# Attention and mixture layer on one core: key columns shared between neighbouring blocks, identities built on chip, second part of the masks loaded later

## The chip, the cores and the metric

The kernel runs on one core of one Trainium2 chip. The metric is the device time of one execution in microseconds (us). A core has a matrix engine (PE, with its weight loads shown as PEld), a vector engine (DVE), a scalar engine (ACT), a general engine (POOL), and a queue engine (SP) that mostly issues DMA transfers. DMAs are issued here by SP, by ACT and by POOL; all of them run on the same 16 DMA engines.

## The reference, cut to what matters

An attention over 8 sequences of 576 positions with 8 heads of 64 channels, followed by a gated layer on the 4608 tokens. Heads 0 to 3 see the last 32 positions, heads 4 to 7 every fourth of the last 128.

```python
def _attn_ref(q, k, v):                       # q, k, v: (8, 8, 576, 64)
    window, dilation = 32, 4
    scores = scale * np.matmul(q, k.transpose(0, 1, 3, 2))
    rel = pos[:, None] - pos[None, :]
    mask_plain = (rel >= 0) & (rel < window)
    mask_dil = (rel >= 0) & (rel < window * dilation) & (rel % dilation == 0)
    ...
    scores = np.where(masks[None], scores, -1000000000.0)
    attn = softmax(scores)
    return np.matmul(attn, v)

def _moe_ref(x, w_gate, w_val, w_out):        # x: 4608 x 512, w_gate and w_val: 512 x 1536, w_out: 1536 x 512
    g = x @ w_gate
    return (silu(g) * (x @ w_val)) @ w_out
```

## The kernel before, in words

**Packs.** The attention is cut into 46 packs. A pack is one pair of heads and up to 512 tokens, cut into blocks of 32 queries. The keys that a block can see are the 32 positions of its own and the 32 before (in steps of four for the dilated heads), so each block reads 64 neighbouring key columns, and blocks that follow each other overlap by 32. `Pack.__init__` lays out the columns of a pack: first the queries, 32 columns a block, then the keys. For each run of blocks (one run for plain heads, four for dilated ones, one for each residue) it keeps 32 more key columns than there are queries. At the start of a sequence the 32 positions before do not exist; their columns hold zeros, and the mask hides them. `cols` is the pack's width, `QKB` the widest (1152 columns), and `qkb`, the array in DRAM, has rows of `QKB` 4-byte columns. `FQ` and `QKB` also set the sizes of buffers, and all buffers that lie behind them.

**Masks and identities.** `masks` holds a 128x128 identity in 16-bit form (`ident16`) and 13 mask tiles of 64 columns. A pack adds the mask to its scores by a matmul of `ident16` with its four mask tiles. `near` marks the first 8 tiles with the identity; those are all that packs 0 to 3 read. `idents` holds two 128x128 identities in 32-bit form, one plain and one with its columns permuted; PE transposes use them (`turn_e`, `turn_y`).

**The start.** Packs 0 to 3 are worked on before any of the layer. Their keys and values lie spread over the partitions with zeros between, so that one matmul serves two heads: `first_qk` loads the queries of a pack (L349, from SP), sets the two halves of its keys to zero (L351), and loads each half into every second partition (L352: one half from SP, one from POOL). `first_v` does the same with the values (L359, L360). The order in which SP, POOL, DVE and ACT issue all this is the order of the code (`manual_schedule`). SP: queries and keys of pack 0, of pack 1, identities (L592), queries and keys of pack 2, values 0, weights unit 0 (`w_load`, L227), values 1, queries and keys of pack 3, values 2, weights unit 1, values 3, weights units 2 to 5. ACT: masks near (L590), a first Exp that loads its table (L593), the rest of the masks (L594). POOL: the zeros and the loads of the second halves, in the same order of packs.

A second list (`"Q0 S0 Q1 Y2 ..."`) gives the order of the work itself on PE, DVE, ACT and POOL. For pack m: `Q` scores (L366 the mask, L370 the blocks), `S` maximum and shift (L377, L378), `X` exponentials (L437), `T` transposes (L441), `K` a copy by ACT (L447), `A` results with the values (L389), `N` normalisation (L396 to L398), `U` transposes back (L475), `H` and `L` the high and low parts of the layer's input (L502, L505). `Y` runs matmuls of no use that keep PE busy, as `idle` does at L583. `W` prepares the weights, unit by unit: `E` (L237) and for some units `T` (L254) on ACT, `T` (L257) and `B` (L264, L267) on DVE, `H` (L275) on ACT, `L` (L279) on POOL.

**The layer.** The first 1536 tokens go through it in three chunks of 512: gate and value products (`gv_mm`, L515), tanh (L524), the gating (L529, L534), output products (L552). The attention of later packs and the preparation of the weights run between. The other 3072 tokens go through a scheme with seven products for eight (L841), whose pieces are mixed, written to DRAM and read again.

Of the kernel before, what the change touches and what calls it, by code (L numbers as in the profile page):

```python
# [18 lines left out]
P = 128  # L19
D = 64  # L20
S = 576
DIL = 4
# [12 lines left out]
BQ = 32  # L35
# [30 lines left out]
class Pack:  # L66


    def __init__(self, chunk, pair, lo, hi):
        self.chunk, self.pair = chunk, pair  # L70
        self.step = DIL if pair >= 2 else 1
        blocks = []
        width = 0
        while lo < hi:
            b, q0 = divmod(lo, S)
            n = min(S - q0, hi - lo)
            per = n // self.step
            nb = -(-per // BQ)
            if self.step == 1:
                blocks += [(b, q0 + BQ * t, BQ, width + BQ * t) for t in range(nb)]  # L80
            else:
                blocks += [(b, q0 + r + DIL * BQ * t, min(BQ, per - BQ * t), width + BQ * ((nb + 1) * r + t))
                           for t in range(nb) for r in range(DIL)]
            width += BQ * (nb + 1) * self.step
            lo += n
        groups = [blocks[a:a + 4] for a in range(0, len(blocks), 4)]
        names = {(1, 0, 0, 0): "a", (0, 0, 1, 0): "b", (1, 1, 1, 1): "F", (0, 0, 0, 0): "o"}
        kinds = "".join(names[tuple(int(q < BQ * self.step) for _, q, _, _ in x)] for x in groups)
        turn = next(n for n in range(len(groups)) if kinds[n:] + kinds[:n] in KINDS)
        self.mask = KINDS.index(kinds[turn:] + kinds[:turn])  # L90
        groups = groups[turn:] + groups[:turn]
        nq = BQ * len(blocks)
        self.groups = [[(b, q, n, BQ * (4 * g + j), nq + k) for j, (b, q, n, k) in enumerate(x)]
                       for g, x in enumerate(groups)]
        self.ng = len(self.groups)
        self.cols = nq + width
        self.order = int(self.step > 1)
        self.runs = []
        for g, x in enumerate(self.groups):
            col, first, n = P * g, S * x[0][0] + x[0][1], sum(y[2] for y in x)  # L100
            if self.runs:
                c, f, k = self.runs[-1]
                if c + k == col and f + k == first:
                    self.runs[-1] = c, f, k + n
                    continue
            self.runs.append((col, first, n))
# [18 lines left out]
NPK = len(PACKS)  # L125
# [4 lines left out]
def block_masks():  # L130

    i, j = np.arange(BQ)[:, None], np.arange(BK)[None, :]
    seen = (j > i) & (j <= i + BQ)
    f, o = [np.where(x, 0.0, NEG) for x in (seen & (j >= BQ), seen)]
    m = dict(o=[o] * 4, F=[f] * 4, a=[f, o, o, o], b=[o, o, f, o])
    return np.concatenate([np.concatenate(m[x]) for x in KINDS], axis=1)


@with_exitstack
def attention_moe(ctx, tc, qkb, vb, w, masks, ident, out):  # L140
    nc = tc.nc
    NS = NPLAIN * NF

# [24 lines left out]
    def at(o, n, dt=F32):  # L168

        assert o % 8 == 0  # L170
        key = o, n, dt
        if key not in named:
            k = n * 4 // mybir.dt.size(dt)
            named[key] = nc.alloc_sbuf_tensor_at(f"at{o}_{n}_{dt.name}", [P, k], dt, offset=origin + 4 * o).ap()
        return named[key]
# [11 lines left out]
    consts = at(0, (NM * BK + P) // 2, BF16)  # L187
    ident16, mask_sb = consts[:, :P], consts[:, P:]

    idents = at(M_SMALL - 2 * P, 2 * P).rearrange("p (n c) -> p n c", n=2)  # L190
# [26 lines left out]
    def w_load():  # L217
        nonlocal loaded
        u = loaded
        n = u % 6 if u < NU - NLAST else (u + 2) % 4  # L220

        if u >= NU or raw_of.get(n, -1) >= done["B"]:
            return False
        raw_of[n] = u
        loaded += 1
        t = at(raw_at[n], 2 * WU, I32)
        last["w"] = nc.sync.dma_start(out=t, in_=w[u // 2, u % 2].bitcast(I32))  # L227
        t = t.rearrange("p (n t) -> p n t", t=2)
        wst[u] = {"lo": t[:, :, 0], "hi": t[:, :, 1]}
        return True  # L230
# [113 lines left out]
    def first_qk(m, *zero):  # L344

        t, n = early["qk"](), pk(m).cols
        k = n - FN
        tk = t[:, FN:FN + 2 * k].rearrange("p (h c) -> p h c", h=2)
        nc.sync.dma_start(out=t[:, :FN], in_=qkb[m, :, :FN])  # L349
        for h in range(2):  # L350
            zero[h].memset(tk[:, h], 0.0)  # L351
            (nc.sync, nc.gpsimd)[h].dma_start(out=tk[h::2, h], in_=qkb[m, D * h:D * h + D, FN:n])  # L352
        st[m]["qk"] = t[:, :FN], tk

    def first_v(m, *zero):
        n = 4 * FG * (D + 1)
        t = early["v"]().rearrange("p (h c) -> p h c", h=2)
        for h in range(2):
            zero[h].memset(t[:, h], 0.0)  # L359
            (nc.sync, nc.gpsimd)[h].dma_start(out=t[h::2, h], in_=vb[m, D * h:D * h + D, :n])  # L360
        st[m]["v"] = t.rearrange("p h (g c) -> p h g c", c=D + 1)
# [215 lines left out]
    near = P + 8 * BK  # L577
# [3 lines left out]
    def idle(n):  # L581
        for _ in range(n):
            nc.tensor.matmul(out=bank_x.rearrange("p (a b) -> p a b", a=4), lhsT=warm,  # L583
                             rhs=warm.unsqueeze(1).broadcast_to([P, 4, P]), start=True, stop=True)

    with tc.manual_schedule(engines={et.SP, et.Pool, et.DVE, et.Activation}):
        nc.vector.memset(ones, 1.0)
        nc.vector.memset(some, 0.0)
        first_qk(0, nc.vector, nc.gpsimd)
        nc.scalar.dma_start(out=consts[:, :near], in_=masks[:, :near])  # L590
        first_qk(1, nc.vector, nc.gpsimd)
        nc.sync.dma_start(out=idents, in_=ident.rearrange("n p c -> p n c"))  # L592
        nc.scalar.activation(out=some, in_=some, func=AF.Exp)  # L593
        nc.scalar.dma_start(out=consts[:, near:], in_=masks[:, near:])  # L594

        idle(WARM)
        first_qk(2, nc.vector, nc.gpsimd)
        first_v(0, nc.vector, nc.gpsimd)
        w_load()
        first_v(1, nc.vector, nc.gpsimd)  # L600
        first_qk(3, nc.gpsimd, nc.gpsimd)
        first_v(2, nc.vector, nc.gpsimd)
        w_load()
        first_v(3, nc.gpsimd, nc.gpsimd)
        for _ in range(3):
            w_load()
        while w_load():
            pass
# [44 lines left out]
    for m in range(M1 + 1, NPK + 1):  # L653
        c, n = divmod(m - M1 - 1, 10)
# [133 lines left out]
    kept = [[at(M_X0 + CS * (4 + 2 * k + r), CS) for r in range(2)] for k in range(2)]  # L788
# [94 lines left out]
    def n_out(ci, t, i):  # L883
        return NT * NP * ci + NP * t + i
# [47 lines left out]
    for ci in range(NC):  # L932
# [20 lines left out]
        for t in range(NT):  # L953
            if ci == NC - 1 and t == NT - 1:
                break
            for i in range(NP):
                n = n_out(ci, t, i)
# [10 lines left out]
                if ci + 1 < NC and slot > 102 and slot % 2 == 0:  # L968
                    k = (slot - 104) // 2
# [3 lines left out]
    t = NT - 1  # L973
# [9 lines left out]
def layout(q, k, v, moe_w_gate, moe_w_val, moe_w_out):  # L983
    qkb = np.zeros((NPK, P, QKB), np.float32)
    vb = np.zeros((NPK, P, 4 * NGM, D + 1), np.float32)
    vb[..., D] = 1.0
    for m, pk in enumerate(PACKS):
        for i, (b, q0, n, qc, kc) in enumerate(x for g in pk.groups for x in g):
            qt = q0 + pk.step * np.arange(n)
            kt = q0 + pk.step * np.arange(-BQ, BQ)  # L990
            a, e = int((kt < 0).sum()), int((kt < S).sum())
            for j in range(2):
                h, r = 2 * pk.pair + j, D * j
                rq = slice(j, P, 2) if m < 4 else slice(r, r + D)
                qkb[m, rq, qc:qc + n] = q[b, h, qt].T
                qkb[m, r:r + D, kc + a:kc + e] = k[b, h, kt[a:e]].T
                vb[m, r + a:r + e, i, :D] = v[b, h, kt[a:e]]
    bits = [np.ascontiguousarray(x).view(np.int64) for x in (moe_w_gate, moe_w_val, moe_w_out)]
    w = np.stack(bits[:2]).reshape(2, NK, P, NF, P)[:, list(ORDER)].reshape(2, 2, 2, P, NF, P)
    w = w.transpose(4, 3, 1, 0, 2, 5).reshape(NF, P, 2 * DM)  # L1000
    w = np.concatenate([w, bits[2].reshape(NF, P, DM)], axis=2)
    w = np.ascontiguousarray(w.reshape(NF, P, 2, WU).transpose(0, 2, 1, 3))
    masks = np.concatenate([np.eye(P), block_masks()], axis=1).astype(ml_dtypes.bfloat16)
    order = np.arange(P).reshape(DIL, BQ).T.ravel()
    ident = np.stack([np.eye(P), np.eye(P)[:, order]]).astype(np.float32)
    return dict(qkb=qkb, vb=vb.reshape(NPK, P, -1), w=w, masks=masks, ident=ident)


_INS = ["qkb", "vb", "w", "masks", "ident"]


# [14 lines left out]
```

## Time and profile before

| | |
|---|---|
| median of 3 runs | 935.71 us (935.17 to 936.23) |
| the profiled execution | 934.96 us, of which its span is 933.2 us |
| PE busy | 921.8 us (99% of the span), 8499 matmuls |
| PEld busy | 751.5 us (81%) |
| DVE, ACT, POOL busy | 639.2, 391.1, 253.8 us |
| DMA | 205.45 MB, mean 220 GB/s |
| granted clock of PE | 1.0 in the whole span |

A row of the timeline gives the start of an instruction in us from the span's start, its duration in us, engine, line, operation, what it writes and reads, and its shape; in brackets stands for how long the engine was idle before it and what ended the wait. A row of the DMA view gives queue, count and size of a group of transfers and the median time from issue to landing in us. "SPq" and "ACTq" are the times at which those engines issue a DMA. A row of the view by stretches gives the length of a stretch and the busy time of PE, PEld, DVE, ACT and POOL in it with the number of instructions, then PE's granted clock, the share of the DMA engines and GB/s.

### The profile page before, as it was taken

The page shows a single profiled execution, that of the slowest core. Times are in us where ns is not written, and L with a number is a line of the kernel's source. Part 1 is how long each engine was busy: PE and PEld are TensorE (multiplying, and loading weights), DVE is VectorE, ACT ScalarE, POOL GpSimd, SP SyncE. Part 2 cuts the span into 40 slices and gives each one's busy share as a digit, 9 for nine tenths or more (in the row PEclk, how much of TensorE's full clock was granted, in tenths as well). Part 3 has the DMA queues.
Part 4 walks back from the last instruction along what each step waited for, and adds up shares of the span by engine and source line. Part 5 has one row for each costly group of instructions (what it writes and reads, how often), then busy time and mean ns, then how long its engine had stood idle before and what let it go on. Part 6 is the DMA issues. An engine that isn't in the chain of part 4 may idle for free.

```text
span 933.2 us, 20559 instructions
## 1 busy us (share of the span) xinstructions
PE 921.8 (99%) x8499; PEld 751.5 (81%) x8499; DVE 639.2 (68%) x1055; ACT 391.1 (42%) x664; POOL 253.8 (27%) x307
## 2 busy tenths in 40 slices
PE   7999999999999999999999999999999999999998
PEld 4778788878888878888888888888888888888886
DVE  6764738668678775757669965666689745656863
ACT  4865623323334233343345643343355523334351
POOL 6655421111111212133223111222223112343320
PEclk9999999999999999999999999999999999999999
DMA  9974515667786980767777778766766686656663
GB/s 349 349 255 174 175 41 198 235 205 262 245 287 217 305 307 5 267 217 222 226 226 236 239 224 255 242 217 213 247 208 195 219 255 189 195 189 195 201 207 111
DMA packets 75533, 205.45 MB, mean 220 GB/s; under 512 B 7728, under 2 KB 22320, under 8 KB 75440
## 3 DMA queue, kind: packets, MB, share of 16 engines
q0 software_dynamic: 27728, 100.77, 34.6%
q1 hardware_dynamic: 35472, 65.16, 19.7%
q10 hardware_dynamic: 12240, 38.20, 11.9%
q8 instruction: 67, 1.10, 0.5%
q14 instruction: 26, 0.21, 0.1%
HBM read 161.64 MB, written 42.47 MB: 219 GB/s over the span
## 4 chain that ended last, share of the span: by engine, by line
PE 73%; DVE 3%; DMA 1%; issue 1%; ACT 1%; SPq 0%; ACTq 0%; DVEq 0%
PE bo L841 32%; PE bv L841 12%; PE bg L841 12%; PE bo L552 4%; PE bg L515 4%; PE bv L515 4%; PE two L457 2%; PE two L417 2%; DMA pieces<-at_float32r 1%; PE two L441 1%; PE two L475 1%; DVE at_float32r L732 0%; SPq L740 0%; DVE at_float L529 0%; DVE at_float L719 0%
## 5 line engine op out<-in xcount | busy, mean ns | idle before, releaser
L841 PE MATMUL bo<-at_float32r 128*128 128x512 f32 x1296 | 307.1, 390 | 0.0
L841 PEld LDWEIGHTS bo<-at_float32r 128*128 128x128 f32 x1296 | 242.2, 188 | 50.6
L770 POOL DMA_DIRECT2D at_float32r<-pieces x189 | 101.3, 536 | 376.7 <-PE bo L841 216.6
L804 DVE TENSOR_TENSOR at_float<-bo,at_float 128x512 f32<-128x512 f32 (+1 forms) x169 | 114.2, 684 | 104.9 <-ACT at_float L846 49.5
L804 DVE TENSOR_TENSOR at_float32r<-at_float,at_float32r 128x512 fp32r<-128x512 f32 (+1 forms) x147 | 114.0, 800 | 40.0 <-ACT at_float32r L831 27.1
L841 PE MATMUL bv<-at_float32r 128*128 128x512 f32 x486 | 129.5, 393 | 0.0
L841 PE MATMUL bg<-at_float32r 128*128 128x512 f32 x486 | 129.3, 392 | 0.0
L515 PE MATMUL bg<-at_float32r,at_float32r 128*128 128x512 f32 x432 | 106.7, 394 | 0.8 <-DVE at_float32r L505 0.4
L515 PE MATMUL bv<-at_float32r,at_float32r 128*128 128x512 f32 x432 | 107.1, 394 | 0.0
L552 PE MATMUL bo<-at_float32r,at_float32r 128*128 128x512 f32 x432 | 106.2, 394 | 0.0
L841 PEld LDWEIGHTS bv<-at_float32r 128*128 128x128 f32 x486 | 90.2, 188 | 19.0
L841 PEld LDWEIGHTS bg<-at_float32r 128*128 128x128 f32 x486 | 90.3, 188 | 18.8
L831 ACT CAST at_float32r<-at_float 128x512 fp32r<-128x512 f32 x126 | 77.0, 622 | 67.4 <-PE bv L841 21.3
L544 POOL TENSOR_TENSOR at_float32r<-at_float,at_float32r 128x512 fp32r<-128x512 f32 x36 | 48.6, 1351 | 204.8 <-PE bo L552 138.3
L515 PEld LDWEIGHTS bg<-at_float32r,at_float32r 128*128 128x128 f32 x432 | 79.9, 188 | 18.8 <-DVE at_float32r L505 1.2
L515 PEld LDWEIGHTS bv<-at_float32r,at_float32r 128*128 128x128 f32 x432 | 79.7, 188 | 17.1 <-DVE at_float L534 0.4
L552 PEld LDWEIGHTS bo<-at_float32r,at_float32r 128*128 128x128 f32 x432 | 79.7, 188 | 16.9
L867 ACT ACTIVATE at_float<-at_float 128x512 f32<-128x512 f32 x72 | 45.6, 633 | 81.7 <-DVE at_float L804 81.7
L846 ACT COPY at_float<-bg 128x512 f32<-128x512 f32 x63 | 37.0, 587 | 94.2 <-PE bg L841 94.0
L529 DVE SCALAR_TENSOR_TENSOR at_float<-at_float,bg 128x512 f32<-128x512 f32 x36 | 24.7, 686 | 66.9 <-ACT at_float L524 66.9
L279 POOL TENSOR_TENSOR at_float32r<-at_int,at_float32r 128x768 fp32r<-128x768 f32 x24 | 44.4, 1858 | 45.2 <-ACT at_float32r L275 45.2
L869 DVE SCALAR_TENSOR_TENSOR at_float<-at_float,at_float 128x512 f32<-128x512 f32 x72 | 49.4, 686 | 10.7 <-ACT at_float L867 10.6
(94 smaller groups left out, 916.4 us busy)
## 6 DMA issues: line engine op xcount, KB each, us to landing
at_float32r<-pieces POOLq DMA_DIRECT2D x189, 512.0 KB, 3.7
pieces<-at_float32r SPq DMA_DIRECT2D x126, 256.0 KB, 3.8
at_int<-w SPq DMA_DIRECT2D x24, 768.0 KB, 7.1
out<-at_float SPq DMA_DIRECT2D x35, 256.0 KB, 3.9
at_float<-vb ACTq DMA_DIRECT2D x15, 520.0 KB, 5.2
at_float<-vb ACTq DMA_DIRECT2D x20, 390.0 KB, 4.7
at_float<-qkb ACTq DMA_DIRECT2D x13, 544.0 KB, 5.7
at_float<-qkb ACTq DMA_DIRECT2D x12, 448.0 KB, 5.2
```

The lines of the kernel that those rows point to most:

```text
L279: nc.gpsimd.tensor_tensor(out=lo, in0=wst.pop(u).bitcast(F32), in1=hi, op=ALU.subtract)
L515: nc.tensor.matmul(out=bank[:, :CH], lhsT=wcol(f, o, low), rhs=x[ORDER[j]], start=n == 0, stop=n == len(ops) - 1)
L529: last["h"] = nc.vector.scalar_tensor_tensor(out=t, in0=t, scalar=1.0, in1=bank_g[:, :CH], op0=ALU.add, op1=ALU.mult)
L544: nc.gpsimd.tensor_tensor(out=hl, in0=hst[i][0], in1=hst[i][1], op=ALU.subtract)
L552: nc.tensor.matmul(out=bank_o[j][:, :CH], lhsT=wcol(f, 2 * DM + P * j, low), rhs=x, start=f == 0 and low == 0 and x is hh, stop=f == NF - ...
L770: nc.gpsimd.dma_start(out=taken[asked], in_=pieces[asked % NPIECE])
L804: engine.tensor_tensor(out=out, in0=a, in1=b, op=op)
L831: nc.scalar.copy(out=o[:, 0], in_=src)
L841: nc.tensor.matmul(out=bank, lhsT=w, rhs=x, start=first and n == 0 and t in FRESH, stop=last and n == len(ops) - 1, skip_group_check=True)
L846: nc.scalar.copy(out=kept[KEPT[t]][r], in_=banks[0][r][:, :CS])
L867: nc.scalar.activation(out=f, in_=g, func=AF.Tanh, scale=0.5)
L869: nc.vector.scalar_tensor_tensor(out=f, in0=f, scalar=1.0, in1=g, op0=ALU.add, op1=ALU.mult)
```

## The change

Three edits.

1. **Columns of keys.** The first block of a sequence no longer has 32 columns of its own for the positions before it. Its first 32 key columns are now those of whatever lies in front: the end of the run before, or, if nothing does, only for the first run of a pack that starts with a sequence, columns of its own. They hold keys that the mask hides. The widest pack goes from 1152 columns to 1056, and `QKB` with it.
2. **Identities.** The array `ident` and its load are gone. ACT makes both 32-bit identities from `ident16`, the second with a permuted access.
3. **Masks.** The second part of the masks is issued by SP behind the values of pack 3, not by ACT behind the first Exp.

```diff
@@ Pack.__init__
-            if self.step == 1:
-                blocks += [(b, q0 + BQ * t, BQ, width + BQ * t) for t in range(nb)]
-            else:
-                blocks += [(b, q0 + r + DIL * BQ * t, min(BQ, per - BQ * t), width + BQ * ((nb + 1) * r + t))
-                           for t in range(nb) for r in range(DIL)]
-            width += BQ * (nb + 1) * self.step
+
+            kept = nb if q0 == 0 else nb + 1
+            k = max(width - BQ, 0) if q0 == 0 else width
+            blocks += [(b, q0 + r + self.step * BQ * t, min(BQ, per - BQ * t), k + BQ * (kept * r + t))
+                       for t in range(nb) for r in range(self.step)]
+            width = k + BQ * (kept * self.step + nb + 1 - kept)
@@ attention_moe
         first_qk(1, nc.vector, nc.gpsimd)
-        nc.sync.dma_start(out=idents, in_=ident.rearrange("n p c -> p n c"))
         nc.scalar.activation(out=some, in_=some, func=AF.Exp)
-        nc.scalar.dma_start(out=consts[:, near:], in_=masks[:, near:])
+        nc.scalar.copy(out=idents[:, 0], in_=ident16)
+        nc.scalar.copy(out=idents[:, 1].rearrange("p (t r) -> p r t", r=DIL),
+                       in_=ident16.rearrange("p (r t) -> p r t", r=DIL))
...
         first_v(3, nc.gpsimd, nc.gpsimd)
+        nc.sync.dma_start(out=consts[:, near:], in_=masks[:, near:])
         for _ in range(3):
             w_load()
@@ layout
-    order = np.arange(P).reshape(DIL, BQ).T.ravel()
-    ident = np.stack([np.eye(P), np.eye(P)[:, order]]).astype(np.float32)
-    return dict(qkb=qkb, vb=vb.reshape(NPK, P, -1), w=w, masks=masks, ident=ident)
+    return dict(qkb=qkb, vb=vb.reshape(NPK, P, -1), w=w, masks=masks)
```

More of the change, by code (lines that the diff above doesn't have):

```diff
@@ L139, in attention_moe @@
 @with_exitstack
-def attention_moe(ctx, tc, qkb, vb, w, masks, ident, out):
+def attention_moe(ctx, tc, qkb, vb, w, masks, out):
     nc = tc.nc
@@ L1003, in layout @@
     masks = np.concatenate([np.eye(P), block_masks()], axis=1).astype(ml_dtypes.bfloat16)
-    order = np.arange(P).reshape(DIL, BQ).T.ravel()
-    ident = np.stack([np.eye(P), np.eye(P)[:, order]]).astype(np.float32)
-    return dict(qkb=qkb, vb=vb.reshape(NPK, P, -1), w=w, masks=masks, ident=ident)
-_INS = ["qkb", "vb", "w", "masks", "ident"]
+    return dict(qkb=qkb, vb=vb.reshape(NPK, P, -1), w=w, masks=masks)
+_INS = ["qkb", "vb", "w", "masks"]
 def kernel(**inputs):
```

## The prediction

> **What bounds the kernel now.** I read the page, then the view by stretches, then the waits of PE, then the timeline of the first 32 us with the DMA rows that belong to it.
>
> ```profile
> span 933.2 us, 20559 instructions
> ```
> ```profile
> 0.00:5.00 5.00, 4.00 (x10) 1.31 (x10) 3.62 (x7) 1.49 (x2) 3.54 (x10) 1.00 0.60 163
> 5.00:31.60 26.60, 21.57 (x322) 14.68 (x320) 19.94 (x35) 17.19 (x26) 14.31 (x17) 1.00 1.02 403
> 31.60:933.20 901.60, 896.18 (x8170) 735.53 (x8170) 615.62 (x1015) 372.45 (x638) 235.97 (x282) 1.00 0.66 215
> ```
> ```profile
> PE two L457 <- DVE at_float32r L489: 1.1, 3, 0.4
> PE two L441 <- ACT at_float L437: 0.7, 1, 0.7
> PE bg L515 <- DVE at_float L529: 0.4, 1, 0.4
> ```
>
> From 31.6 us on PE is busy for 896.18 of 901.60 us, at the full granted clock, and the waits of PE in that part are these three rows, 2.2 us, none of them for a DMA. So there PE is the bound, and what the change does to later loads (fewer key columns in most of 46 packs) is hidden under PE. The first 31.6 us are another matter: PE idles 26.60 - 21.57 = 5.03 us of the second stretch, and there the share of the DMA engines is 1.02, that is, they are full. Whatever comes out of this change comes out of the start, and moves all that follows by as much.
>
> How the start hangs together, from its timeline:
>
> ```profile
> 6.63 1.08 PE L370 MATMUL fs<-at_float 128*32 128x128 f32 x32 [1.19 <-DMA at_float<-qkb]
> ...
> 12.05 0.59 ACT L447 COPY at_float<-fk 128x512 f32<-128x512 f32 x1 [0.29 <-PE fk L441]
> ...
> 13.62 1.09 PE L389 MATMUL fr<-at_float,at_float 128*32 128x130 f32 x32 [1.15 <-POOL at_float L359]
> ...
> 16.11 1.09 PE L389 MATMUL fr<-at_float,at_float 128*32 128x130 f32 x32 [0.81 <-DVE at_float L398]
> ...
> 19.09 0.69 DVE L377 TENSOR_REDUCE at_float<-fs 128x8 f32<-128x512 f32 x1 [0.69 <-PE fs L370]
> ...
> 27.90 0.68 DVE L505 TENSOR_TENSOR at_float32r<-fs,at_float32r 128x512 fp32r<-128x512 f32 x1
> ...
> 31.58 0.50 PE L515 MATMUL bg<-at_float32r,at_float32r 128*128 128x512 f32 x1 [0.41 <-DVE at_float L529]
> ```
>
> The first scores wait for keys. The results of pack 0 (13.62) are put down to POOL's zeros (L359), but those had long been done; by the issue and landing rows below it is a DMA. After the results of pack 1 (16.11) PE works nearly without a gap to the scores of pack 3, whose maximum on DVE starts at 19.09; from there DVE runs without a pause to the low part of pack 3 at 27.90, after which the layer starts and PE is full from 31.58. So the end is set by how early the chain 13.62, 16.11, 19.09 runs.
>
> Issues by POOL (start, us) and the DMA rows of the same transfers (landing after so many us), in the same order: keys of pack 0, values of pack 0, values of pack 1.
>
> ```profile
> 1.69 0.67 POOL L352 DMA_DIRECT2D at_float<-qkb  x1 [0.32 <-POOL at_float L351]
> ...
> 6.55 0.54 POOL L360 DMA_DIRECT2D at_float<-vb  x1 [0.30 <-POOL at_float L359]
> ...
> 8.36 0.54 POOL L360 DMA_DIRECT2D at_float<-vb  x1 [0.29 <-POOL at_float L359]
> ```
> ```profile
> at_float<-qkb POOLq DMA_DIRECT2D x1, 160.0 KB, 4.6
> at_float<-vb POOLq DMA_DIRECT2D x1, 260.0 KB, 6.8
> at_float<-vb POOLq DMA_DIRECT2D x1, 260.0 KB, 7.5
> ```
>
> Keys 0 land at 1.69 + 4.6 = 6.29, and the scores start at 6.63. Values 0 land at 6.55 + 6.8 = 13.35, and their use starts at 13.62, although the copy that it also needs ended at 12.05 + 0.59 = 12.64. Values 1 land at 8.36 + 7.5 = 15.86, and their use starts at 16.11, together with the end of the normalisation before it. Three gates of the start are loads on full DMA engines.
>
> **The change part by part.** *The identities' load goes.* It is issued by SP right behind the keys of pack 1; both rows and their landings:
>
> ```profile
> 2.86 0.48 SPq L352 DMA_DIRECT2D at_float<-qkb  x1
> ...
> 3.38 0.59 SPq L592 DMA_DIRECT2D at_float<-ident  x1
> ```
> ```profile
> at_float<-qkb SPq DMA_DIRECT2D x1, 136.0 KB, 4.6
> ```
> ```profile
> at_float<-ident SPq DMA_DIRECT2D x1, 128.0 KB, 5.3
> ```
>
> Keys 1 land at 7.46, the identities at 8.68: on SP's queue they take up to 1.22 us, which is the upper end. The lower end is their 131 KB at the rate of a full stretch (354 GB/s, below): 0.37 us. Later issues of SP come 0.6 us earlier, which costs nothing and gives nothing, as the queue behind them is full already.
>
> ```profile
> 5.90:6.90 1.00, 0.27 (x12) 0.30 (x16) 0.24 (x1) 0.00 (x0) 0.70 (x2) 1.00 1.09 354
> ```
> ```profile
> q10 hardware_dynamic: 288, 0.25, 18.6%
> ```
>
> The second row is ACT's DMA queue in the first 4 us: both parts of the masks, 246 KB in short packets, took 0.186 x 4 = 0.74 us of all DMA engines. By that rate 131 KB cost 0.39 us. Short packets of masks are the nearest row to the short rows of the identities (512 bytes), so I take 0.39 us.
>
> *The second part of the masks moves.* It is a third of those bytes and half of the packets: 0.25 to 0.37 us less ahead of the keys and values; I take 0.25, by bytes as before. It comes back behind values 3, ahead of weights units 2 to 5: one more issue on SP (about the 0.59 us of the identities' row) and 0.25 us of DMA. Behind it wait these weights alone. They land earlier by all the rest of the sum and later by this 0.25; the exponent step on ACT waits for one of them:
>
> ```profile
> 25.83 0.94 ACT L237 ACTIVATE at_int<-at_int 128x768 f32<-128x768 f32 x1 [0.49 <-DMA at_int<-w]
> 26.66 0.56 ACT L502 CAST at_float32r<-fs 128x512 fp32r<-128x512 f32 x1
> ```
>
> The high part of pack 3 stands behind it on ACT and ends at 27.22, 0.68 us ahead of the DVE step at 27.90 that reads it. That slack covers the 0.25. If it did not, the loss would be those 0.25 us at most. The masks themselves are first read by later packs, beyond this stretch.
>
> *Fewer key columns.* Among the first four packs only 0 and 2 (dilated) shrink, by 96 columns of 4 bytes in 128 rows: 49 KB each, 98 KB together, at 354 GB/s 0.28 us. The zeros shrink as well:
>
> ```profile
> L351 DVE MEMSET at_float<- 128x640 f32 x2 | 1.2, 592 | 0.2
> ...
> L351 DVE MEMSET at_float<- 128x544 f32 x1 | 0.5, 512 | 0.1
> ```
>
> 0.08 us on DVE for each pack; POOL does its halves, so its later issues come some 0.15 us earlier. On a full queue that adds nothing to the DMA term, and I do not add it.
>
> [...] Rows of the array go from 4608 bytes (18 x 256) to 4224 (16.5 x 256), so every second row starts off a 256-byte boundary. The rows of the values have 4160 bytes, three of four off such a boundary, and the DMA rows of later packs do not show it as a loss:
>
> ```profile
> at_float<-vb ACTq DMA_DIRECT2D x15, 520.0 KB, 5.2
> ...
> at_float<-qkb ACTq DMA_DIRECT2D x13, 544.0 KB, 5.7
> ```
>
> I take nothing for it. [...]
>
> *ACT's copies.* Two copies of 128x128; the nearest row and the next thing that ACT does for the start:
>
> ```profile
> L497 ACT COPY at_float<-two 128x128 f32<-128x128 f32 x6 | 1.7, 284 | 0.0
> ```
> ```profile
> 9.22 0.63 ACT L437 ACTIVATE at_float<-at_float 128x512 f32<-128x512 f32 x1 [6.54 <-DVE at_float L378]
> ```
>
> Two such copies are 0.57 us. They wait for the near masks, which the masks' matmul on PE also needs well ahead of 6.63. Behind them on ACT stands the exponential at 9.22, with 6.54 us idle ahead of it: even copies slowed threefold by the permuted access cost nothing. Their reader, the transposes ahead of the copy at 12.05, comes later still.
>
> *Sum.* Ahead of values 0 and 1 the DMA engines have 0.39 + 0.25 + 0.28 = 0.92 us less to do. Upper end: 1.22 + 0.37 + 0.28 = 1.87, but the results of pack 0 also need the copy that ends at 12.64. That moves only with the first scores; ahead of them lie the 0.25 to 0.37 of the masks and half of the keys' 0.28, some 0.4 to 0.5 us. So the results can start at about 12.1 at best, 1.5 us earlier, and that caps the gain. Lower end: the 0.15 us of POOL's earlier issues. The later gates (values 1 at 15.86, the work of DVE from 19.09 on) move alike. I take 0.9 us. Against the profiled execution: 934.96 - 0.9 = 934.1 us. The median is 0.75 above that execution, so 935.71 - 0.9 = 934.8 us.
>
> What this measurement can tell from no change is about 0.2%, 1.9 us; so I forecast a small gain that counts as no change.
>
> **The rivals.** *POOL's queue keeps its own pace* (0.20). The gates are loads of POOL's queue, the bytes removed lie mostly on SP's and ACT's. [...] For it: values 0 take 6.8 us to land while a weights unit is under way. Against it: the engines are full, and in a full stretch work that is gone must come off something. [...]
>
> *All gates give way* (0.08). The identities' 1.22 us fall wholly to POOL's queue and the first scores move by 1 us as well, so that the cap is gone: at least 1.9 us, 933.8 or below, faster. Against it: the keys of pack 0 are issued ahead of the identities.
>
> *PE's order gets worse* (0.06). The layer's matmuls are cut into by attention work where the scheduler finds it ready, and loads of other lengths could move the cuts.
>
> ```profile
> 207.94 2.95 PE bv L515 x12
> 210.89 2.72 PE bo L552 x12
> ```
> ```profile
> 40.13 2.20 PE L515 MATMUL bg<-at_float32r,at_float32r 128*128 128x512 f32 x9
> ```
>
> Twelve matmuls take 2.72 us, and 2.95 after a cut, so a cut costs 0.23; the last row shows a set of twelve cut after nine. To be slower by over 1.9 us with 0.9 gained takes (1.9 + 0.9) / 0.23 = 13 cuts more: 937.6. Against it: 46 packs have their places in the code, and all their loads are issued long before use.
>
> **How the numbers follow.** The forecast has 0.66. Forecast and first rival stay within 0.2%: 0.86; faster 0.08; slower 0.06. The range takes in the forecast's ends (0.15 to 1.5 us gained), the first rival, and 0.5 us either way for the spread of the runs: 933.7 to 936.1.
>
> **What would show it.** Right: no transfer of identities; the first scores near 6.2, the results of pack 0 near 12.7, of pack 1 near 15.2, DVE's maximum near 18.2, and the layer's full pace from 30.7, with the same idle time of PE as before after that. The first rival shows as values 0 landing near 13.2 again. Wrong: a wait of PE behind the copies of ACT, or for the weights that stand behind the moved masks, or more than 5.5 us of idle PE after the start.

## The result and the profile after

The changed kernel took 940.60 us (median of 6 runs, 939.92 to 940.98), the kernel before 935.44 us beside it (6 runs, 934.51 to 936.23). The ratio is 1.0054, with a 95% interval from 1.0041 to 1.0067: slower by 5.2 us. The profiled execution took 940.98 us. Its page, the span and the line of the engines:

```profile
span 939.2 us, 20559 instructions
...
PE 923.2 (98%) x8499; PEld 753.0 (80%) x8499; DVE 638.6 (68%) x1055; ACT 391.7 (42%) x666; POOL 253.4 (27%) x307
```

The span grew by 6.0 us, while the count of instructions is the same. The view by stretches, with the cuts used for before (stretch and its length, then the busy time of PE, weight loads, DVE, ACT and POOL, then granted clock, DMA share and GB/s):

```profile
5.00:31.60 26.60, 18.10 (x307) 12.77 (x308) 16.38 (x29) 13.32 (x20) 12.13 (x15) 0.99 0.96 378
31.60:933.20 901.60, 898.96 (x8175) 737.42 (x8174) 617.98 (x1018) 376.28 (x643) 237.77 (x283) 1.00 0.65 214
```

In the start, PE did 18.10 us of work where before did 21.57, so it idled 8.50 us instead of 5.03. The other engines did less there too (DVE 16.38 for 19.94, ACT 13.32 for 17.19): the whole start waited for something. The timeline of the start shows where it turns from ahead to behind:

```profile
6.15 1.08 PE L370 MATMUL fs<-at_float 128*32 128x128 f32 x32 [1.34 <-POOL at_float L359]
...
13.22 1.09 PE L389 MATMUL fr<-at_float,at_float 128*32 128x130 f32 x32 [1.09 <-DMA at_float<-vb]
...
15.60 1.09 PE L389 MATMUL fr<-at_float,at_float 128*32 128x130 f32 x32 [0.70 <-issue]
...
18.57 0.69 DVE L377 TENSOR_REDUCE at_float<-fs 128x8 f32<-128x512 f32 x1 [0.69 <-PE fs L370]
18.72 1.73 POOL L279 TENSOR_TENSOR at_float32r<-at_int,at_float32r 128x768 fp32r<-128x768 f32 x1 [4.37 <-ACT at_float32r L275]
...
20.40 0.56 POOL L360 DMA_DIRECT2D at_float<-vb  x1
24.90 1.72 POOL L279 TENSOR_TENSOR at_float32r<-at_int,at_float32r 128x768 fp32r<-128x768 f32 x1 [3.94 <-ACT at_float32r L275]
...
27.32 1.09 PE L389 MATMUL fr<-at_float,at_float 128*32 128x130 f32 x32 [1.82 <-POOL at_float32r L279]
...
31.84 0.68 DVE L505 TENSOR_TENSOR at_float32r<-fs,at_float32r 128x512 fp32r<-128x512 f32 x1
...
36.44 3.02 PE L515 MATMUL bg<-at_float32r,at_float32r 128*128 128x512 f32 x12 [0.26 <-DVE at_float L529]
```

Up to 18.57 every step stands 0.4 to 0.5 us earlier than in the kernel before: the first scores at 6.15 for 6.63, the results of pack 0 at 13.22 for 13.62, those of pack 1 at 15.60 for 16.11, DVE's maximum of pack 3 at 18.57 for 19.09. Then POOL's queue holds something unexpected. POOL waits 4.37 us with nothing to do, subtracts to make the low part of weights unit 0 (L279) from 18.72, and only then issues, at 20.40, the load of the second half of values 3 (L360). In the kernel before the same load, and the results that need it:

```profile
14.79 0.54 POOL L360 DMA_DIRECT2D at_float<-vb  x1 [0.30 <-POOL at_float L359]
...
22.78 1.09 PE L389 MATMUL fr<-at_float,at_float 128*32 128x130 f32 x32
```

The rows of the load itself (KB, then us from issue to landing), before and after:

```profile
at_float<-vb POOLq DMA_DIRECT2D x1, 260.0 KB, 6.1
```
```profile
at_float<-vb POOLq DMA_DIRECT2D x1, 260.0 KB, 6.8
```

Before: issued at 14.79, landed at 20.89, used at 22.78, with 1.9 us to spare. After: issued at 20.40, landed at 27.20, used at 27.32. The results of pack 3 start 4.54 us later, although the load is 6.31 us later. The bracket of the row at 27.32 names POOL's L279, and the waits of PE repeat it:

```profile
PE fr L389 <- POOL at_float32r L279: 1.8, 1, 1.8
```

It is not L279 that ends this wait: the subtraction that ended last before it began at 24.90 and ended at 26.62, and the results started 0.12 us after the landing. A wait that names an engine long done is to be checked against the DMA rows.

Behind pack 3's results, its low part starts on DVE at 31.84 (27.90 before, 3.94 later), and the layer is at full pace, with its first set of twelve products run in one go, at 36.44 (31.58 before, 4.86 later). So another 0.92 us is lost between the two, where the stretch by single microseconds shows the granted clock (the number ahead of the DMA share):

```profile
31.00:32.00 1.00, 0.89 (x3) 0.69 (x4) 1.00 (x3) 1.00 (x2) 0.00 (x0) 0.66 0.12 49
32.00:33.00 1.00, 1.00 (x4) 0.73 (x3) 1.00 (x2) 1.00 (x2) 0.00 (x0) 0.50 0.26 25
33.00:34.00 1.00, 1.00 (x4) 0.81 (x3) 1.00 (x2) 0.86 (x2) 0.64 (x1) 0.50 0.52 117
34.00:35.00 1.00, 1.00 (x4) 0.76 (x4) 0.25 (x1) 0.26 (x1) 1.00 (x1) 0.63 1.00 418
```

The clock falls to 0.50. What is missing adds up to 0.34 + 0.50 + 0.50 + 0.37 = 1.71 us, which is 3.4 us at half clock, just where the layer's first products run; before had 1.00 there. What makes it fall there is not shown: ahead of the fall, from 28.0 to 31.3, PE was busy for 1.48 of 3.30 us at a clock of 1.00.

Of the 6.0 us of span, 4.86 are made by 36.44. The other 1.2 lie in the 900 us behind the start, which took 902.8 us here (939.2 less 36.44) and 901.6 before. It will be seen below that this part scatters by more than that from one profile to the next. In the medians 5.2 - 4.9 = 0.3 us is left.

So the load stands behind a subtraction that waits for ACT. In the code it does not. All issues of the start stand in a first list, in manual order, and the work in a second one; the load of values 3 is the last of POOL's first list, and the subtraction for unit 0 the first of its second. The order in which the built program holds POOL's instructions (number, line, operation, output and input), before:

```
20 L359 MEMSET at_2080_float_194 128x1040 x2
21 L360 DMA at_2080_float_194<-vb 64x1040
22 L279 ISA
23 L279 TENSOR_TENSOR at_1536_float32r<-at_776_int_313,at_1536_float32r 128x768
```

and after:

```
20 L359 MEMSET at_2080_float_194 128x1040 x2
21 L279 ISA
22 L279 TENSOR_TENSOR at_1536_float32r<-at_776_int_314,at_1536_float32r 128x768
23 L360 DMA at_2080_float_194<-vb 64x1040
```

Within each list the order is that of the code, but across the border between the two the program was built with the two instructions swapped. No line of the diff touches either of them.

### The profile page after: what moved, and what is told of

Read it like the earlier page. It is cut to its first block, busy times and chain, and to the rows that moved or that the text cites. A ratio compares the mean times of both kernels' runs of the same rounds, so it can differ in the third digit from the quotient of the medians.

```text
span 939.2 us, 20559 instructions
## 1 busy us (share of the span) xinstructions
PE 923.2 (98%) x8499; PEld 753.0 (80%) x8499; DVE 638.6 (68%) x1055; ACT 391.7 (42%) x666; POOL 253.4 (27%) x307
## 4 chain that ended last, share of the span: by engine, by line
PE 73%; DVE 3%; DMA 1%; issue 1%; ACT 1%; SPq 0%; ACTq 0%; DVEq 0%
PE bo L843 31%; PE bv L843 12%; PE bg L843 12%; PE bo L552 4%; PE bg L515 4%; PE bv L515 4%; PE two L457 2%; PE two L417 2%; DMA pieces<-at_float32r 1%; PE two L441 1%; PE two L475 1%; DVE at_float32r L734 0%; SPq L742 0%; DVE at_float L529 0%; DVE at_float L721 0%
## 5 line engine op out<-in xcount | busy, mean ns | idle before, releaser
L279 POOL TENSOR_TENSOR at_float32r<-at_int,at_float32r 128x768 fp32r<-128x768 f32 x24 | 43.4, 1817 | 52.5 <-ACT at_float32r L275 48.5
```

The costliest lines, as they stand in the source:

```text
L279: nc.gpsimd.tensor_tensor(out=lo, in0=wst.pop(u).bitcast(F32), in1=hi, op=ALU.subtract)
```

## The experiments

The first theory: the whole loss is this swap, made by the identities' edit, and with the order restored the three edits gain what the prediction said, or nothing. Its rivals: the loss comes from the load's place but also from the edits' other effects (ACT's copies, moved masks), or from the masks' and columns' edits.

### The order pinned

The changed kernel, with the subtraction ordered behind the last load of the first list:

```
-            (nc.sync, nc.gpsimd)[h].dma_start(out=t[h::2, h], ...)
+            last["v"] = (nc.sync, nc.gpsimd)[h].dma_start(out=t[h::2, h], ...)
...
-        nc.gpsimd.tensor_tensor(out=lo, ..., op=ALU.subtract)
+        with tc.issue_after(last["v"].ins):
+            nc.gpsimd.tensor_tensor(out=lo, ..., op=ALU.subtract)
```

> The changed kernel with one edge added on POOL: the first weights' subtraction (unit 0, low part) stays behind the load of the second half of values 3, as it was before the change. Theory 'order on POOL' (the load of values 3 is issued at 20.40 us behind the subtraction where it was issued at 14.79 before, so the results of pack 3 start at 27.3 for 22.8): the loss is gone, and the 0.5 us that the earlier steps gained are left: 934.5 to 935.3 us, faster than the kernel after by 5 to 6 us. Rival 'masks on SP' (the moved masks hold up the weights behind them): no more than 1 us better than the kernel after, about 940. Rival 'copies on ACT or columns off a 256-byte boundary': about 940 too.

Measured: 935.62 us (12 runs) beside 935.18 for before; ratio 1.0003, interval 0.9994 to 1.0012. Its timeline (lines are one higher from here on):

```profile
13.73 1.09 PE L390 MATMUL fr<-at_float,at_float 128*32 128x130 f32 x32 [1.40 <-ACT at_float L438]
...
14.63 0.54 POOL L361 DMA_DIRECT2D at_float<-vb  x1 [0.29 <-POOL at_float L360]
...
22.77 1.09 PE L390 MATMUL fr<-at_float,at_float 128*32 128x130 f32 x32
...
31.57 3.04 PE L516 MATMUL bg<-at_float32r,at_float32r 128*128 128x512 f32 x12 [0.39 <-DVE at_float L530]
```

The load is issued at 14.63 again, and all that follows stands as before, to 31.57 for 31.58. The order is the whole loss. But the gain is not there either (the 934.5 to 935.3 us expected were missed): the results of pack 0 start at 13.73, and values 0 landed at 13.49 (issued 6.39, 7.1 us later), not earlier than before's 13.35. The same kernel once more in the third set of runs:

> The pinned kernel once more, beside the two others on the same chip: 935.2 to 936, within 0.1% of the kernel before.

Measured: 935.34 us (11 runs) beside 935.21; 0.9999, 0.9990 to 1.0008. Values 0 landed at 13.19.

### The identities' edit alone, and the other two without it

The kernel before with only the second edit:

```
-        nc.sync.dma_start(out=idents, in_=ident.rearrange("n p c -> p n c"))
...
+        nc.scalar.copy(out=idents[:, 0], in_=ident16)
+        nc.scalar.copy(out=idents[:, 1].rearrange("p (t r) -> p r t", r=DIL),
+                       in_=ident16.rearrange("p (r t) -> p r t", r=DIL))
```

> Only the second edit: identities by ACT, no identities' load; columns and masks as before. In the built order of POOL the subtraction stands ahead of the load of values 3 here too. Theory 'order on POOL': slow, 939.5 to 941. Rival 'masks on SP': about 935, as the masks are not moved. Rival 'columns': about 935.

And the changed kernel with the identities loaded again (the reverse of that diff), that is, columns and masks alone:

> Only the first and third edits: shared key columns and masks' second part on SP; identities loaded as before. The built order of POOL is that of the kernel before. Theory 'order on POOL': 934.8 to 935.6, no slower than the kernel before. Rival 'masks on SP': 938 to 941. Rival 'columns off a 256-byte boundary': 938 to 941.

Measured: 940.61 us with the identities' edit alone (4 runs; 1.0054, 1.0037 to 1.0071), and 935.79 us with the other two (12 runs; 1.0004, 0.9995 to 1.0013), both beside 935.18. The load of values 3 and the layer's full pace, first with the identities' edit alone, then with the other two:

```profile
20.86 0.56 POOL L360 DMA_DIRECT2D at_float<-vb  x1
...
36.00 3.03 PE L515 MATMUL bg<-at_float32r,at_float32r 128*128 128x512 f32 x12 [0.35 <-DVE at_float L529]
```
```profile
14.64 0.54 POOL L360 DMA_DIRECT2D at_float<-vb  x1 [0.30 <-POOL at_float L359]
...
31.81 3.03 PE L515 MATMUL bg<-at_float32r,at_float32r 128*128 128x512 f32 x12 [0.39 <-DVE at_float L529]
```

One edit turns the order and loses 5 us; the other two leave it and are worth nothing that can be measured (935.79 lies just above the 934.8 to 935.6 expected).

### The kernel before with a late load

None of the edits, but the load held back until the subtraction for unit 0 is issued:

```
+            if m == 3 and h == 1:
+                held.append(t)
+            else:
...
+        "D": lambda m: nc.gpsimd.dma_start(out=held[0][1::2, 1], in_=vb[m, D:2 * D, :4 * FG * (D + 1)]),
...
-        ... U1 W4 A2 H1 ...
+        ... U1 W4 D3 A2 H1 ...
```

> The kernel before, none of the three edits, with the order on POOL turned round by hand: the load of the second half of values 3 is issued behind the first subtraction of the weights. Theory 'order on POOL': slower by 4.5 to 6.5 us, 940 to 942. Rivals: 935 to 936, as nothing else is changed.

Measured: 941.54 us (4 runs); 1.0063, 1.0043 to 1.0082.

```profile
20.38 0.57 POOL L624 DMA_DIRECT2D at_float<-vb  x1
...
27.26 1.09 PE L394 MATMUL fr<-at_float,at_float 128*32 128x130 f32 x32 [0.19 <-issue]
...
36.43 3.06 PE L520 MATMUL bg<-at_float32r,at_float32r 128*128 128x512 f32 x12 [0.22 <-DVE at_float L534]
```

Issue, use and full pace stand within 0.06 us of the changed kernel's 20.40, 27.32 and 36.44. With the pinned kernel this shows it from both sides: the late load alone makes the loss, and its removal takes all of it away.

### The copies on DVE

What in the edit turns the order? In programs that were only built, not run, the order turned whenever the identities' load left SP's queue (also when ACT issued it instead), unless the copies were put on DVE; with the load kept on SP it stayed as before. With one issue less, weights unit 0 is issued at 5.07 us (6.51 before), so a scheduler that orders by when it takes an instruction to be ready would see the subtraction sooner. The runs without a pin fit it: the order is turned where unit 0 is issued at 5.07 or 5.17 us (the latter with the identities' edit alone), and as before at 5.59 (the other two edits), 6.51 and 6.66 (the run below). That is an argument from orders, and no run shows the scheduler's reckoning. The run that goes with it, the changed kernel with

```
-        nc.scalar.copy(out=idents[:, 0], in_=ident16)
-        nc.scalar.copy(out=idents[:, 1]...
+        nc.vector.tensor_copy(out=idents[:, 0], in_=ident16)
+        nc.vector.tensor_copy(out=idents[:, 1]...
```

> The kernel after, with the two identity copies on DVE and not on ACT, and no edge on POOL. The built order of POOL has the load of values 3 ahead of the subtraction again, as it stands before the change. Theory 'order on POOL': 935 to 936. Rival 'masks on SP' or 'columns': about 940, as both edits are still in.

Measured: 936.40 us (10 runs) beside 935.80; 1.0008, 0.9999 to 1.0018. That is 0.4 us above the range expected.

```profile
14.64 0.54 POOL L360 DMA_DIRECT2D at_float<-vb  x1 [0.29 <-POOL at_float L359]
...
16.64 1.33 PE L389 MATMUL fr<-at_float,at_float 128*32 128x130 f32 x32 [2.45 <-DMA at_float<-vb]
```

The order is back, and the loss gone, without a pin and with the identities still made on the chip. So it is not the copies as such that cost the 5 us, but the order. (Its profiled execution, 938.33 us, is the longest of its ten: values 1 landed late there, PE idled for 2.45 us, and its clock had a mean of 0.59 from 17 to 19 us. More on its loads follows under "Where the gain went".)

### What the half clock costs

The changed kernel with five matmuls of no use behind pack 3's normalisation, where PE has little to do:

```
+    def fill(n):
+        for _ in range(n):
+            nc.tensor.matmul(out=s_banks[1], lhsT=ident16, rhs=consts[:, :512], start=True, stop=True)
+    first["I"] = fill
...
-        ... L0 W2 W0 N3 W3 W4 ...
+        ... L0 W2 W0 N3 I5 W3 W4 ...
```

> The kernel after (values 3 late), with five matmuls of no use on PE between the results of pack 3 and its transposes back, where PE idles from 28.4 to 29.7 us. In the kernel after the granted clock is 0.50 from 32 to 34 us and the first gate products take 2.21 us for five where they take 1.41 at full clock; from the low part of pack 3 to the full pace it takes 4.6 us for 3.7 before. Theory 'the late load costs twice, by the wait and by the clock that falls in it': the clock stays at 1.0, those 0.9 us come back, 939.5 to 940. Rival 'the wait alone': no gain, 940.6, or a loss of up to 0.5 us if the filling gets in the way.

Measured: 941.27 us (5 runs) beside 935.80; 1.0065, 1.0053 to 1.0077. Not faster than the changed kernel. Its stretches:

```profile
24.00:25.00 1.00, 1.00 (x4) 0.75 (x3) 0.41 (x1) 0.81 (x2) 0.00 (x0) 0.50 0.99 412
...
26.00:27.00 1.00, 1.00 (x3) 0.75 (x3) 0.00 (x0) 0.11 (x1) 1.00 (x1) 0.50 1.01 419
...
33.00:35.00 2.00, 1.96 (x8) 1.61 (x9) 1.71 (x2) 1.82 (x3) 1.22 (x1) 1.00 0.60 175
```
```profile
27.78 1.09 PE L389 MATMUL fr<-at_float,at_float 128*32 128x130 f32 x32 [0.27 <-issue]
...
35.99 1.20 PE L515 MATMUL bg<-at_float32r,at_float32r 128*128 128x512 f32 x4 [0.35 <-DVE at_float L529]
```

The clock was full from 33 to 35, and from pack 3's results to full pace it took 8.21 us where the changed kernel took 9.12, so 0.91 less. But half clock came earlier, from 24 to 27. This is not the filling's doing. The five matmuls start at 28.81, behind that half clock, and the run with the identities' edit alone, which has the late load and no filling, shows the same place and the same 8.21 us (27.79 to 36.00):

```profile
24.00:25.00 1.00, 1.00 (x4) 0.80 (x3) 0.40 (x1) 0.81 (x2) 0.00 (x0) 0.50 1.03 423
```
```profile
27.79 1.09 PE L389 MATMUL fr<-at_float,at_float 128*32 128x130 f32 x32 [0.29 <-issue]
```

So the half clock falls now here, now there, with the same late load, and what the filling does to it stays open. The results of pack 3 start 0.46 us later in the filled run because their load is issued 0.47 later (20.87 for 20.40). With the half clock behind pack 3's results the way from there to full pace takes 9.12 us (9.17 in the kernel before with a late load), with the half clock ahead of them 8.21. That 0.9 us of the profiled loss are the clock's is read from these traces; in the time no run shows it, and the expectation was missed. Nor does the loss need it: two of the changed kernel's six executions have a mean clock of 1.0, where 1.71 us missing would make 0.998, and they took 940.68 and 939.92 us.

### Where the gain went

With the order restored the start should have been 0.9 us shorter. One thought was that weights unit 0, which now lands at 12.37 (13.71 before), took what the other loads left. So it was moved behind values 1, in the pinned kernel and in the kernel before (with the pin):

```
         first_v(0, nc.vector, nc.gpsimd)
-        w_load()
         first_v(1, nc.vector, nc.gpsimd)
+        w_load()
```

> The kernel of the run with the order on POOL pinned, and SP issues weights unit 0 behind its half of values 1 and not ahead of it. There the second half of values 0 (POOL's queue) still landed at 13.49 us, no earlier than before, though 0.3 MB less was loaded ahead; unit 0 was issued 1.4 us earlier and landed at 12.47 for 13.71. Theory 'the freed time went to unit 0': with unit 0 later, values 0 land at 12.6 or before, the results of pack 0 start near 12.6, and the time is 0.5 to 1.0 us below that run (934.6 to 935.1). Rival 'POOL's queue keeps its own pace whatever SP has queued': values 0 land at 13 to 13.5 again and the time is the same, 935.6.

> The kernel before with the same move of unit 0 behind values 1, and with POOL's order pinned as it is built there anyway; none of the three edits. Theory 'the freed time went to unit 0': the kernel before gains less than the changed one from the move, since there unit 0 is issued late already: 0 to 0.5 us, 934.7 to 935.4. Rival 'the move is worth the same in both': as much below the kernel before as the other run is below the pinned one.

Measured: 936.38 us (12 runs; 1.0010, 1.0000 to 1.0020) and 936.20 us (11 runs; 1.0010, 1.0001 to 1.0019), both beside 935.80. The results of pack 0 in the first, and of pack 1 in the second:

```profile
13.36 1.09 PE L390 MATMUL fr<-at_float,at_float 128*32 128x130 f32 x32 [1.67 <-DMA at_float<-vb]
```
```profile
16.50 1.09 PE L390 MATMUL fr<-at_float,at_float 128*32 128x130 f32 x32 [1.49 <-DMA at_float<-vb]
```

Both expectations, 934.6 to 935.1 and 934.7 to 935.4 us, were missed. Values 0 landed at 13.09 and 13.05, within the 12.85 to 13.49 of all but one of the other runs that issue this load at 6.39 to 6.56 us. That thought falls. The exception is the run with the copies on DVE, where the load, issued at 6.39, landed at 11.49:

```profile
at_float<-vb POOLq DMA_DIRECT2D x1, 260.0 KB, 5.1
```

There DVE's zeros from pack 2's keys on stand behind the copies, and SP's loads behind these zeros: SP's half of values 0 is issued at 6.14 (4.43 in the pinned run), unit 0 at 6.66 (5.07). Values 1 landed at 16.41 in return (14.51 in the pinned run), and nothing was gained. So POOL's own pace is not the whole of it; what the other queues hold at the time seems to count, and no run separates which of their loads it is. The other thought: the landing follows the issue, at POOL's own pace. POOL issues values 0 only after it has set their second half to zero, so the zeros were given to DVE, in the pinned kernel and in the kernel before (with the pin):

```
-        first_v(0, nc.vector, nc.gpsimd)
+        first_v(0, nc.vector, nc.vector)
```

> The pinned kernel (all three edits, order on POOL as before), and DVE sets both halves of values 0 to zero, so that POOL issues its half some 1.2 us earlier (near 5.1 for 6.39 us). In seven profiles so far that load landed 6.3 to 7.1 us after its issue, whatever had been taken from the queues. Theory 'the load goes by its issue on POOL': values 0 land near 11.8, the results of pack 0 start near 12.5 (then held by ACT's copy), the layer's full pace comes 0.8 to 1.2 us earlier, and the time is 934.4 to 935.0. Rival 'the DMA engines are full and it lands when they get to it': values 0 land at 12.8 to 13.5 as before, no gain, 935.6. Rival 'another step holds the start': values 0 land early and the low part of pack 3 still starts at 27.9, no gain.

> The kernel before with the same step for values 0 and with the edge on POOL, none of the three edits. Theory 'the load goes by its issue on POOL': the same gain as with the edits, 934.4 to 935.0; so the edits themselves are worth nothing there. If the engines' load counts, values 0 land 0.5 us later here than with the edits and the gain is half.

Measured: 934.93 us (0.9999, 0.9990 to 1.0008) and 934.72 us (0.9994, 0.9985 to 1.0004), 11 runs each, beside 935.21. The pinned kernel:

```profile
5.15 0.54 POOL L361 DMA_DIRECT2D at_float<-vb  x1
...
11.88 1.09 PE L390 MATMUL fr<-at_float,at_float 128*32 128x130 f32 x32 [0.46 <-ACT at_float L448]
...
30.54 3.03 PE L516 MATMUL bg<-at_float32r,at_float32r 128*128 128x512 f32 x12 [0.35 <-DVE at_float L530]
```

and its row of the load:

```profile
at_float<-vb POOLq DMA_DIRECT2D x1, 260.0 KB, 6.6
```

Issued 1.24 us earlier than in the first pinned run, the load landed at 11.75, 1.74 earlier, and full pace came at 30.54, 1.03 earlier (beside the second pinned run 1.44 and 0.78). The earlier issue moved the gate; the bytes that the edits took off the other queues did not. In the kernel before the load landed at 11.15, but in that profile the first scores ran at about half speed (the view by stretches gives a clock of 1.00 there, so the cause is open):

```profile
6.71 1.71 PE L371 MATMUL fs<-at_float 128*32 128x128 f32 x26 [1.27 <-DMA at_float<-qkb]
...
13.83 1.09 PE L390 MATMUL fr<-at_float,at_float 128*32 128x130 f32 x32 [0.21 <-ACT at_float L448]
...
31.68 3.00 PE L516 MATMUL bg<-at_float32r,at_float32r 128*128 128x512 f32 x12 [0.36 <-DVE at_float L530]
```

so that ACT's copy for pack 0 became the late one, and nothing was gained. The two medians are the lowest of all kernels, by 0.3 and 0.5 us beside before's, but both intervals hold 1: a faster version is not shown. The second time falls in the range expected without the earlier full pace that was to bring it, which is luck.

What lies behind the layer's full pace took (span less the row of full pace) 901.2 us in the last kernel, 901.6 in before, 902.6 in the one with its zeros on DVE, 902.9 in the first pinned run, 902.8 in the changed one and 904.9 in the one with the late load. The last has a second fall of the clock, from 342 to 346 us, with 1.71 us missing once more:

```profile
343.00:344.00 1.00, 1.00 (x4) 0.81 (x3) 1.00 (x3) 0.84 (x3) 0.96 (x2) 0.50 0.80 265
```

Most of these 900 us are the same program. So one profile settles a microsecond of the start, but not one of the whole, and the rest of the scatter was not followed further.

## Why the prediction was wrong

It said 934.8 us, range 933.7 to 936.1, and gave 0.06 to slower. Measured was 940.60.

**The step that failed** is in the paragraph on the identities' load: "Later issues of SP come 0.6 us earlier, which costs nothing and gives nothing, as the queue behind them is full already." The issues did come earlier (unit 0 at 5.07 for 6.51), and the program was built in another order. The prediction took POOL's order to be that of the code, from the zeros and loads of the first list to the work of the second. Its own term for POOL, "its later issues come some 0.15 us earlier", held for values 2 (11.92 for 12.08) and failed for values 3 (20.40 for 14.79). It costed the removed issue as time on SP's queue and did not ask what order the program would get without it. What the runs showed in its place: the second half of values 3 is issued behind a subtraction that waits for ACT until 18.72, lands 6.31 us later, and costs 5.2 us. The prediction had looked at the issue rows of keys 0, values 0 and values 1; the row of 14.79, with the 1.9 us that values 3 had to spare, was not asked for.

**The sum** failed as well, unseen under the loss. The 0.92 us of DMA work were to come off ahead of values 0 and 1, since "in a full stretch work that is gone must come off something". Values 0 landed 6.6 us (changed kernel), 7.1 and 6.8 us (pinned, two runs) after their issue, and 6.8 before. With the order restored the time is before's: 1.0003 and 0.9999; 0.9 us less would be 0.9990, outside the first interval and at the edge of the second. The first rival, POOL's queue at its own pace, is what the pinned runs agree with: with the 0.15 us of POOL's earlier issues as the whole gain, 935.71 - 0.15 = 935.56 us stand beside their 935.62 and 935.34, and its sign, values 0 landing near 13.2, beside their 13.49 and 13.19. What sets this pace no run shows, and it is not fixed: with the copies on DVE the load took 5.1 us. Weights unit 0 landed 1.34 us earlier, so some of the freed time went there, but moving it away did not bring it to values 0.

**The rivals on the slow side.** "PE's order gets worse" looked for a turned order in the layer, on PE; it was turned on POOL, in the start, and one load was enough for what it priced at 13 cuts.

**What held.** What the change does lies in the start, as far as the scatter behind it lets one tell: the load of identities is gone, ACT's copies are hidden. They run at 3.90 and 4.11 us:

```profile
3.90 0.30 ACT L593 CAST at_float<-at_bfloat 128x128 f32<-128x128 bf16 x1 [1.22 <-DMA at_bfloat<-masks]
4.11 0.42 ACT L594 CAST at_float<-at_bfloat 128x128 f32<-128x128 bf16 x1
```

The permuted copy takes 0.42 for the plain one's 0.30, where up to threefold was allowed for. Columns and moved masks cost nothing, and gave nothing (1.0004). Of the signs named beforehand, "more than 5.5 us of idle PE after the start" tells nothing: behind full pace PE idled 6.07 us (902.76 less 896.69) for 5.42 before, but 4.78 to 6.47 in the kernels that lost nothing. The loss showed in the start itself, 8.50 for 5.03, for which no sign was set.

## What to carry to other kernels

Where two stretches of hand-ordered code meet, the order across the border belongs to the scheduler, and an edit that removes one issue on one queue can turn it on another; so read from the built program, per engine, which loads stand behind an instruction that waits, and pin the border. POOL's load of values 3 was only as early as the instruction ahead of it (issued at 20.40 us behind the subtraction, at 14.79 where it stood ahead of it): ask for the slack of every load of that queue, not just of the ones that gate now. On full DMA engines (a share of 1.01 from 5 to 31.6 us in the first pinned run), issuing values 0 1.24 us earlier brought its landing 1.74 us earlier; taking an estimated 0.92 us of work off ahead of it did not, and a landing that came earlier where other loads came later (values 0 at 11.49 for 13.49) was paid for by the next load (values 1 at 16.41 for 14.51).

## What the runs showed of the hardware

Values 0, a load of 260 KB on POOL's queue, landed 5.1 to 7.1 us after its issue in the thirteen profiles. At nearly the same issue time (6.39 to 6.56 us) the landing scattered between 12.85 and 13.49 us in ten of them, and came at 11.49 in the one with the copies on DVE, where SP's loads were issued later.

In six falls of the granted clock, in five profiles and at four different places, it missed the same amount, 1.70 to 1.71 us in each. One is from 31 to 35 us in the changed kernel, another from 23 to 28 with five idle matmuls added behind it:

```profile
23.00:24.00 1.00, 0.40 (x1) 0.36 (x2) 1.00 (x2) 1.00 (x2) 0.00 (x0) 0.89 1.01 418
...
27.00:28.00 1.00, 0.73 (x10) 0.25 (x12) 0.00 (x0) 0.00 (x0) 0.10 (x1) 0.90 1.06 442
```

There it is 0.11 + 3 x 0.50 + 0.10 = 1.71. In the run with the identities' edit alone the fall at the same place followed 3.40 us (20.5 to 23.9) in which PE was busy for 2.12; in the changed kernel PE was busy for 2.13 of the same 3.40 us, and the clock stayed at 1.00 from 22 to 31. So how busy PE was there does not tell the two apart. The same late load had its fall at 23 to 28 us in two profiles and at 31 to 35 in two others; where it comes in executions without a profile isn't shown.
